# A transformer block on one core: gate and up of the last but one tile as whole matmuls, TensorE's instruction blocks in the planner's clock, and a rule row for each 64 banks

## The chip, the cores and the metric

The kernel runs on one core of a Trainium2 chip. The metric is the device time of one execution in microseconds, as the median of several runs. The profile is a recording of one execution; its lines name the engines PE (TensorE, with PEld for its weight loads), DVE (VectorE), ACT (ScalarE), POOL (GpSimd) and SP (SyncE, which issues the DMAs).

## The reference

One block of a transformer, with 2048 tokens of width 512, 32 heads of 16 columns and a feed-forward part of width 1792, all in bfloat16:

```python
mod = (silu(c) @ w_mod)                 # six rows of 512: sa, ca, ga, sb, cb, gb
h = layernorm(x) * (1 + ca) + sa
q, k, v = h @ wqkv                      # 32 heads, 16 columns each
p = softmax(q @ k.T / 4)                # 32 x 2048 x 2048 exponentials
x = x + ga * ((p @ v) @ wo)
h = layernorm(x) * (1 + cb) + sb
x = x + gb * ((gelu(h @ w_gate) * (h @ w_up)) @ w_down)
```

The 134 million exponentials are the bulk of what ScalarE does.

## The kernel before

**Tiling.** The queries are cut into seven sets (`SETS`): two of 512 tokens, three of 256 and two of 128. For every set the heads are taken in eight groups of four; for each group and each block of keys TensorE writes scores to a bank of PSUM, 128 keys by 512 columns (`qk`). A bank is the unit in which the kernel counts (`pos`). Six banks `ps_sc` hold scores, in two halves of three (`CH`). The bank `ps_pv` collects the product of the exponentials with the values (`pv_mms`), and `ps_mi` serves side work; late in the kernel the sixth score bank serves side work too (`bank`).

**Exponentials.** ScalarE turns two or three banks at a time into `E` (L369 in the profile). A part of the banks goes to VectorE: one `TENSOR_SCALAR` a bank writes the bits of an approximate power into `mreg` or `dreg`, and for four such banks three more operations on 2048 columns follow (`power_task`: mantissa, square, exponent); such a group is a "quad" in the code. Its product with the values takes two passes of 16 matmuls where a group of ScalarE's takes one.

**Side work.** Projections, the output projection with `wo`, the second normalisation and the feed-forward part of the sets that are done run on TensorE between the scores. With `split` set, `mm` writes a matmul of 128 weight columns as four of 32 columns, placed side by side on the array; with `whole` it stays one. Every matmul of the program is followed through two instructions, the weight load and the product. The last set but one (tile 14) is treated apart: `side_last` transposes its normalised rows (L354), then `side_raw` computes gate and up in eight chunks (`raw_chunk`), and VectorE copies each chunk from PSUM into `hreg`. GeLU, the product and the down projection of that tile follow behind the last exponential, in `tail`, beside the last tile's whole chain: sums, output projection, normalisation, gate, up, down. There gate and up of the last tile are whole matmuls already, since `tail` clears `split`.

**What sets the order.** No order is written out. The program is generated by a planner, `stream`, that keeps a clock of its own: `model` gives each operation a cost, and at every step the loop asks whether the next scores can start, whether a product with values is ready, whether side work is due and paid for (`credit`), or whether a filler matmul should run, one whose result isn't used. `plan` gives side work its windows, from `DUE` and the end of each set. Thresholds for all this stand in `RULES`, a row of nine numbers for a stretch of banks: readiness margin, the tolerated hole on VectorE, VectorE's allowed backlog, how far ScalarE may be ahead before scores go to VectorE alone, the columns that TensorE should have done in the last 3413 ns of the planner's clock (below that, fillers run), and so on. What the planner decides is then fixed in the program: each engine runs its own list in order and waits on semaphores for the others.

The model of a matmul, cut:

```python
cols, rows, tp = cost
mode = 0 if tp is None else (1 if rows == 32 else 2)
t = max(t, self.pe_issue)
if mode != self.pe_mode:
    t = max(t, self.pe_end + 105)
```

Of the kernel before, what the change touches and what calls it, by code (L numbers as in the profile page):

```python
# [21 lines left out]
NDC = D // P  # L22
NFC = F // P
NKT = S_TOK // P
# [8 lines left out]
QS = 2  # L33
PEN = {NSET - 2: (6, 7), NSET - 1: (5, 6, 7)}
NRAW = 8
CH = 3
SC = 2 * CH
NSL = 27
assert NSL % CH == 0
LEAD = 5  # L40
# [3 lines left out]
NEAR = 8  # L44
FIRST = 0
LAST = 3
FLOW = 4
DUE = (1054, 1420, 1597, 1802, -12, 0, -20)


def WIN(ends):
    due = DUE[:4] + (ends[5] + DUE[4], ends[5] - 16 + DUE[5], ends[6] + DUE[6])
    res = []
    for k in range(NSET - 2):
        s0 = max(ends[k] + 33, due[k - 1] if k else 0)
        res += [(s0, min(due[k], s0 + 15 * SETS[k][1] // P)), (s0, due[k])]
    return res + [(due[5], due[5]), (due[5], due[6])]
# [2 lines left out]
URGENT = 12  # L60
LATE = 2
RULES = (
# [16 lines left out]
)  # L79
END = (0, None)  # L80

# [13 lines left out]
_Rule = collections.namedtuple("_Rule", "ready hole back fill lag early alone ahead side2")  # L95


class _Op:
    __slots__ = ("eng", "stream", "seq", "fn", "inc", "waits", "clock", "tag", "t1")

    def __init__(self, eng, stream, seq, fn):
        self.eng = eng
        self.stream = stream
        self.seq = seq
        self.fn = fn
        self.inc = False
        self.waits = {}
        self.clock = None
        self.tag = None


class _Recorder:


    def __init__(self, nc):
        self.nc = nc
        self.ops = []
        self.count = {}
        self.bystream = {}
        self.clock = {e: {} for e in ALLENG}  # L120
        self.hist = {}
        self.pitch = {}
        self.kind = {}
        self.sem = {}
        self.dry = False
        self.split = False
        self.gelu = False
        self.probing = None
        self.free = {e: 700.0 for e in ALLENG}
        self.dma_free = self.pe_issue = self.pe_end = 0.0  # L130
        self.pe_mode = None
        self.tile_free = [0.0] * 16
        self.log = []

    def sb(self, name, shape, dt):
# [67 lines left out]
    def rec(self, eng, fn, reads=(), writes=(), dma=None, cost=0.0):  # L203

        if self.dry:
            return None
        stream = eng if dma is None else "d_" + dma
        seq = self.count.get(stream, 0) + 1
        needs = {}

# [70 lines left out]
    def model(self, op, t, cost):  # L281
        eng = op.eng
        if op.stream not in COMPUTE:
            size, run = cost
            self.free[eng] = t + 450
            self.dma_free = max(t + 900, self.dma_free) + size / (320 if run >= 1024 else 245 if run >= 512 else 200)
            op.t1 = self.dma_free + (1000 if run > 64 else 1500) + (1200 if self.split and size < 65536 else 0)
        elif eng == "pe":
            cols, rows, tp = cost
            mode = 0 if tp is None else (1 if rows == 32 else 2)  # L290
            t = max(t, self.pe_issue)
            if mode != self.pe_mode:
                t = max(t, self.pe_end + 105)
            q = range(16)
            if mode == 1:
                q = range(tp[0] // 8, tp[0] // 8 + 4)
            elif mode == 2:
                q = range(tp[1] // 32, 16, 4)
            t = max(t, max(self.tile_free[i] for i in q))
            end = t + max(cols, 64) / 2.4  # L300
            for i in q:
                self.tile_free[i] = end
            self.pe_mode, self.pe_issue, self.pe_end = mode, t + (4 if mode else 27), max(self.pe_end, end)
            self.free[eng] = t
            self.log.append((t, cols if mode == 0 else cols / 4))
            op.t1 = end + 158
        else:
            self.free[eng] = t + cost
            op.t1 = t + cost + (self.lag if eng == "act" else 92)
# [152 lines left out]
class _Kernel(_Recorder):  # L462
# [271 lines left out]
    def side_proj(self, col, g, fin):  # L734
# [5 lines left out]
        fin(mi)  # L740
        yield END

# [15 lines left out]
    def side_v(self, g, dc):  # L758
# [12 lines left out]
        self.done(("v", g, dc))  # L771
        yield END

    def side_t(self, src, n, h, out, mod):
# [9 lines left out]
        for i in range(2):  # L784
            dc = 2 * h + i
            self.modulate("dve", out(dc), pt[:, w * i:w * i + w], mod, dc)
        yield END

# [49 lines left out]
    def side_mod(self):  # L838
# [5 lines left out]
        for dst, k, s in ((self.ga, 2, 1.0), (self.gb, 5, 1.0)):  # L844
# [3 lines left out]
            self.ts("dve", dst[:, :], mi, s, None, ALU.mult)  # L848
            yield END
        for ci in range(0, 8, 2):  # L850
# [4 lines left out]
        if not self.dry:  # L855
            self.task([lambda qd=qd: self.tt("dve", self.wo[:, qd, :], self.wo[:, qd, :], self.ga[:, :], ALU.mult)
                       for qd in range(8)], "wo")
        yield END

# [5 lines left out]
    def side_wo_load(self):  # L865
# [7 lines left out]
        for j in range(4):  # L873
            for ee in range(2):
                src = self.A_wo.rearrange("(a j e r) n -> j e r a n", j=4, e=2, r=DH)[j, ee]
                self.dma("sp", self.wo[32 * j:32 * j + DH, ee:8:2, :], src, "wo%d" % (2 * j + ee))
        yield END

# [36 lines left out]
        self.tt("dve", self.xs[:, t, :], self.xs[:, t, :], self.xw, ALU.add)  # L915
        self.dma("sp", self.out[0, P * t:P * t + P, :], self.xs[:, t, :], "out%d" % (t % 4))

    def up_mm(self, bank, w, fc, c0, W, dci):
        self.mm(bank, self.up_w(w, fc, dci), self.t2T[:, dci, c0:c0 + W], start=(dci == 0), stop=(dci == NDC - 1))

    def near_end(self, k, qd, den):

# [35 lines left out]
    def side_ffn(self, gi, begin=False):  # L958
# [5 lines left out]
        prod = self.prodT if W == 512 else self.prodL  # L964
        flow = gi < FLOW
        kpb = 512 // W
# [89 lines left out]
    def raw_chunk(self, k, i, mi):  # L1056

        W, c0 = SETS[k][1], BCOL[k]
        x, f0 = i // 4, i % 4 * 4
        n = min(4, NFC - f0)  # L1060
        for s in range(n):
            for dci in range(NDC):
                yield W, lambda s=s, dci=dci: self.up_mm(
                    mi[:, W * s:W * s + W], (self.wg, self.wu)[x], f0 + s, c0, W, dci)
        dst = (self.gate5, self.up5)[x][:, f0:f0 + n, :]
        return lambda eng: self.copy(eng, dst, mi[:, 0:W * n].rearrange("p (k n) -> p k n", k=n))

    def side_raw(self, k):
        for i in range(NRAW):
            f = yield from self.raw_chunk(k, i, self.bank())  # L1070
            f("dve")
            self.done(("raw", k, i))
            yield END
# [134 lines left out]
    def stream(self):  # L1208
# [11 lines left out]
        rounds = []  # L1220
# [23 lines left out]
        pos = c = e = rp = loaded = 0  # L1244
# [8 lines left out]
        self.plain = dict(left)  # L1253
        quads = []
        wait = []
        cand = [k for k, (u, r, g0) in enumerate(rounds) if FIRST <= r < NKT * u[3] // 512 - LAST]
        self.begun = lambda u: group[u] <= cg
        quad = None

        def take(n):  # L1260
            r, i = [], pos
            while len(r) < n and i < nseq:
                if i not in vec:
                    r.append(i)
                i += 1
            return r, i

        def pick(q):
            used = [seq[m][2] for m in take(CH - 1)[0]]
            return next((q["rnd"][2] + j for j in q["j"] if j not in used), None)  # L1270

        def overdue():
            return {x[1][1] for x in self.tasks if x[1] is not None and x[1][0] == "shift" and self.plain[x[1][1]] <= LATE}
# [128 lines left out]

        early, late = self.weight_parts()
        while cg <= group[units[-1]]:
            self.rule = _Rule(*RULES[min(pos // 128, len(RULES) - 1)])
            parts = early or late
            if parts and pos >= loaded and (pos >= ends[FLOW - 1] + 8 if early else ("ffn", FLOW - 1) in self.have):
                parts.pop(0)()
# [3 lines left out]
            t = max(self.pe_now(), virt)  # L1412
# [4 lines left out]
            if c % 2:  # L1417
                self.two = self.fifth or (pos >= TWO_AT(ends) and self.credit > self.rule.side2)
            mem, after = take(CH - 1 if (left[units[1]] or self.two) and c % 2 else CH)
            s0 = CH * (c % 2)  # L1420
            if mem:
# [3 lines left out]
            if tq is not None and tq <= t + self.rule.ready:  # L1425
                slack = self.free["act"] - 600 - t
                w = self.next_side()
# [6 lines left out]
                if self.free["act"] > t + self.rule.alone and self.free["dve"] < t + 1500 and ("k", 3, 0) in self.have:  # L1434
                    alone = []
                    while len(alone) < CH:
                        if quad is None and not new_quad(overdue()):
# [43 lines left out]
                pos, e, c = after, e0 + n, c + 1  # L1481
# [4 lines left out]
            w = self.next_side()  # L1486
# [185 lines left out]
    def tail_rest(self, k, down):  # L1672
        q0, W = SETS[k]
        for i in range(NRAW, 8):
            gen = self.raw_chunk(k, i, self.scp[:, i % 3, :])
# [127 lines left out]
```

## Time and profile before

| what | value |
|---|---|
| median of three runs | 827.08 us (826.73 to 829.11) |
| the profiled execution | 827.44 us |
| its span, first to last instruction | 825.7 us |
| ScalarE busy | 795.3 us |
| VectorE busy | 754.5 us |
| TensorE busy | 753.6 us, 14256 matmuls |
| exponentials from scores on ScalarE | 451 of two banks, 246 of three |

The span is the time from the first instruction to the last; the execution's own time lies 1.74 us above it. A line of a group names the line of the program (often that of a helper), the engine, the operation, output and inputs by name, the shape and the number of instructions, then busy time in us and the mean of one in ns, and what ended the idle time before them. In a timeline a line gives the start in us, the length, and in brackets how long the engine had been idle and what it had waited for; "issue" means that it waited for nothing that the profile shows. Instructions of a group overlap, so that the mean of one may be longer than its share of the busy time.

### The profile page before, as it was taken

The page shows a single profiled execution, that of the slowest core. Times are in us where ns is not written, and L with a number is a line of the kernel's source. Part 1 is how long each engine was busy: PE and PEld are TensorE (multiplying, and loading weights), DVE is VectorE, ACT ScalarE, POOL GpSimd, SP SyncE. Part 2 cuts the span into 40 slices and gives each one's busy share as a digit, 9 for nine tenths or more (in the row PEclk, how much of TensorE's full clock was granted, in tenths as well). Part 3 has the DMA queues.
Part 4 walks back from the last instruction along what each step waited for, and adds up shares of the span by engine and source line. Part 5 has one row for each costly group of instructions (what it writes and reads, how often), then busy time and mean ns, then how long its engine had stood idle before and what let it go on. Part 6 is the DMA issues. An engine that isn't in the chain of part 4 may idle for free.

```text
span 825.7 us, 31347 instructions
## 1 busy us (share of the span) xinstructions
PE 753.6 (91%) x14256; PEld 303.8 (37%) x14256; DVE 754.5 (91%) x1359; ACT 795.3 (96%) x742; POOL 4.5 (1%) x13
## 2 busy tenths in 40 slices
PE   7999999989998998999898989998999999999977
PEld 3333333322222222222333333343543344465654
DVE  7866999999999999999998999999999999798755
ACT  6999999999999999999999999999999999999972
POOL 2000000000000000000000000000000000000000
PEclk9999999999999999999999999999999999999999
DMA  8101000000003211110003212111662433500000
GB/s 281 53 2 36 10 9 10 10 10 10 6 6 100 58 46 35 47 35 15 22 13 92 65 51 57 51 28 33 185 169 56 112 98 86 152 20 16 13 10 14
DMA packets 77215, 43.78 MB, mean 53 GB/s; under 512 B 21269, under 2 KB 75482, under 8 KB 77082
## 3 DMA queue, kind: packets, MB, share of 16 engines
q1 hardware_dynamic: 77080, 41.78, 18.4%
q8 instruction: 111, 1.82, 0.9%
q14 instruction: 22, 0.18, 0.1%
q10 hardware_dynamic: 2, 0.00, 0.0%
HBM read 39.15 MB, written 2.60 MB: 51 GB/s over the span
## 4 chain that ended last, share of the span: by engine, by line
ACT 83%; PE 11%; DVE 2%; DMA 1%; SPq 1%; issue 1%; DVEq 0%
ACT E L369 80%; PE ps_sc L350 6%; PE ps_mi L350 3%; ACT hreg L369 2%; PE ps_pv L350 1%; ACT L369 1%; SPq L419 1%; DMA xs<-in_A_x_dram 1%; DVE mreg L381 0%; DMA rb<-scr_rec 0%; DVE hreg L373 0%; DVE wreg L373 0%; DVE wreg L381 0%; DVE mreg L373 0%; DVE osb L390 0%
## 5 line engine op out<-in xcount | busy, mean ns | idle before, releaser
L369 ACT ACTIVATE E<-ps_sc 128x1024 bf16<-128x1024 f32 (+1 forms) x701 | 749.0, 1292 | 10.7 <-PE ps_sc L350 10.4
L350 PE MATMUL ps_sc<-qT,kmo 32*128 32x256 bf16 (+2 forms) x1728 | 199.2, 294 | 21.4 <-ACT E L369 17.8
L350 PE MATMUL ps_sc<-qT,kme 32*128 32x256 bf16 (+2 forms) x1728 | 195.5, 294 | 24.0 <-ACT E L369 18.6
L381 DVE TENSOR_SCALAR mreg<-ps_sc 128x512 uint16<-128x512 f32 x256 | 171.3, 686 | 11.9 <-PE ps_sc L350 9.9
L350 PE MATMUL ps_pv<-E,vaug 128*17 128x256 bf16 (+2 forms) x2720 | 148.5, 291 | 0.9 <-DVE osb L390 0.5
L350 PE MATMUL ps_mi<-wreg,mreg 128*32 128x256 bf16 (+2 forms) x1888 | 107.2, 325 | 4.9 <-DVE hreg L373 1.2
L350 PEld LDWEIGHTS ps_sc<-qT,kme 32*128 32x128 bf16 x1728 | 57.8, 92 | 142.4 <-ACT E L369 115.8
L350 PEld LDWEIGHTS ps_sc<-qT,kmo 32*128 32x128 bf16 x1728 | 58.6, 92 | 129.0 <-ACT E L369 106.8
L381 DVE TENSOR_SCALAR dreg<-ps_sc 128x512 uint16<-128x512 f32 x152 | 102.1, 686 | 3.1 <-PE ps_sc L350 1.7
L350 PEld LDWEIGHTS ps_pv<-E,vaug 128*17 128x17 bf16 x2720 | 53.8, 90 | 54.5 <-issue 38.0
L381 DVE TENSOR_SCALAR mreg<-mreg 128x2048 uint16<-128x2048 uint16 x96 | 65.0, 682 | 0.1
L350 PEld LDWEIGHTS ps_mi<-wreg,mreg 128*32 128x32 bf16 x1888 | 40.8, 95 | 46.5 <-issue 20.9
L350 PE MATMUL ps_pv<-mreg,vaug 128*17 128x256 bf16 (+2 forms) x816 | 48.0, 299 | 1.7 <-DVE mreg L373 1.0
L350 PE MATMUL ps_mi<-hreg,wreg 128*32 128x512 bf16 x480 | 38.5, 385 | 1.1 <-DVE vaug L390 0.9
L373 DVE TENSOR_TENSOR dreg<-mreg,dreg 128x2048 bf16<-128x2048 bf16 x32 | 38.9, 1216 | 0.1
L373 DVE TENSOR_TENSOR mreg<-dreg,mreg 128x2048 bf16<-128x2048 bf16 x32 | 38.7, 1211 | 0.1
L373 DVE TENSOR_TENSOR mreg<-mreg 128x2048 bf16<-128x2048 bf16 x32 | 38.8, 1212 | 0.0
L390 DVE CAST hreg<-ps_mi 128x512 bf16<-128x512 f32 (+1 forms) x50 | 33.8, 675 | 4.4 <-PE ps_mi L350 3.9
L350 PE MATMUL ps_mi<-xs,ident 128*32 128x512 bf16 (+2 forms) x424 | 33.1, 376 | 2.1 <-DMA xs<-in_A_x_dram 1.1
L350 PE MATMUL ps_mi<-wo,onorm 128*32 128x512 bf16 x448 | 33.6, 383 | 0.4 <-DVE onorm L373 0.2
L350 PE MATMUL ps_pv<-dreg,vaug 128*17 128x256 bf16 (+2 forms) x528 | 29.7, 290 | 3.0 <-DVE dreg L373 1.8
L373 DVE TENSOR_TENSOR hreg<-ps_mi,hreg 128x512 bf16<-128x512 f32 x44 | 30.2, 687 | 0.9 <-PE ps_mi L350 0.5
(170 smaller groups left out, 699.5 us busy)
## 6 DMA issues: line engine op xcount, KB each, us to landing
mreg<-in_B_w_up_dram SPq DMA_DIRECT2D x32, 256.0 KB, 3.0
mreg<-in_B_w_gate_dram SPq DMA_DIRECT2D x28, 256.0 KB, 3.4
mreg<-in_B_w_down_dram SPq DMA_DIRECT2D x16, 256.0 KB, 2.9
dreg<-in_B_w_down_dram SPq DMA_DIRECT2D x12, 256.0 KB, 3.3
mreg<-in_w_mod_dram SPq DMA_DIRECT2D x1, 2048.0 KB, 12.8
rb<-scr_rec SPq DMA_DIRECT2D x64, 32.0 KB, 1.9
out_dram<-xs SPq DMA_DIRECT2D x16, 128.0 KB, 1.7
rb<-scr_rec SPq DMA_DIRECT2D x104, 16.0 KB, 1.8
```

The lines of the kernel that those rows point to most:

```text
L350: return self.rec("pe", lambda e: e.matmul(out, lhsT, rhs, start=start, stop=stop, tile_position=tp), [lhsT, rhs, *after], [out], cost=(n, ...
L369: return self.rec("act", lambda e: e.activation(out, in_, func, scale=scale, **kw), rd, wr, cost=self.cost("act", out, [in_], "act") + load)
L373: return self.rec(eng, lambda e: e.tensor_tensor(out, a, b, op), [a, b], [out], cost=self.cost(eng, out, [a, b], "tt"))
L381: return self.rec(eng, lambda e: e.tensor_scalar(out, a, s1, s2, **kw), rd, [out], cost=self.cost(eng, out, [a], "ts") + (60 if len(rd) > ...
L390: return self.rec(eng, lambda e: e.tensor_copy(out, in_), [in_], [out], cost=self.cost(eng, out, [in_], "ts"))
L419: return e.dma_start(out, in_)
```

## The change

It has four parts.

1. `raw_chunk`, gate and up of tile 14 in the stream, asks for whole matmuls (`WHOLE`): one of 128 weight columns in place of four of 32.
2. The planner's clock counts TensorE's instructions, two for a matmul. At every 256 of them (`BLOCK`, the first after 63 have been counted ahead, `HEAD`) the next matmul may not start sooner than 3650 ns (`FETCH`) after the start of the block before.
3. `RULES` is read by `pos // 64` and not `pos // 128`, and its 16 rows become 31, most with new numbers.
4. The due time of tile 14's output projection is 34 banks earlier (`DUE`). `LASTW` is an empty table: the choice of groups for VectorE reads it, and falls back to `LAST` as before.

```diff
+WHOLE = True
+LASTW = {}
-DUE = (1054, 1420, 1597, 1802, -12, 0, -20)
+DUE = (1054, 1420, 1597, 1802, -12, -34, -20)
 RULES = (
-    (30, 450, 8, 4200, 1536, 400, 3200, 20, 1800),
+    (30, 50, 8, 2700, 1536, 400, 3200, 20, 1800),
+    (80, 100, 8, 4200, 1536, 400, 3200, 20, 2500),
...
+SEGB = 64
+HEAD, BLOCK, FETCH = 63, 256, 3650.0
...
+        self.pe_count, self.pe_block = HEAD, 0.0
...
             t = max(t, self.pe_issue)
+            self.pe_count += 2
+            if self.pe_count >= BLOCK:
+                self.pe_count -= BLOCK
+                t = self.pe_block = max(t, self.pe_block + FETCH)
             if mode != self.pe_mode:
...
-    def up_mm(self, bank, w, fc, c0, W, dci):
-        self.mm(bank, self.up_w(w, fc, dci), self.t2T[:, dci, c0:c0 + W], start=(dci == 0), stop=(dci == NDC - 1))
+    def up_mm(self, bank, w, fc, c0, W, dci, whole=False):
+        self.mm(bank, self.up_w(w, fc, dci), self.t2T[:, dci, c0:c0 + W], start=(dci == 0), stop=(dci == NDC - 1), whole=whole)
...
-                    mi[:, W * s:W * s + W], (self.wg, self.wu)[x], f0 + s, c0, W, dci)
+                    mi[:, W * s:W * s + W], (self.wg, self.wu)[x], f0 + s, c0, W, dci, WHOLE)
...
-        cand = [k for k, (u, r, g0) in enumerate(rounds) if FIRST <= r < NKT * u[3] // 512 - LAST]
+        cand = [k for k, (u, r, g0) in enumerate(rounds) if FIRST <= r < NKT * u[3] // 512 - LASTW.get(u[3], LAST)]
...
-            self.rule = _Rule(*RULES[min(pos // 128, len(RULES) - 1)])
+            self.rule = _Rule(*RULES[min(pos // SEGB, len(RULES) - 1)])
```

What the planner makes of it, first on TensorE, in the middle of tile 14's gate. `wreg` holds the transposed rows, `qT` and `hreg` by then hold weights of gate (the queries in that part of `qT` are used up), `ps_mi` and one bank of `ps_sc` collect the chunks, and rows with `kme` are scores. Before:

```order
L350 MATMUL ps_sc<-wreg,qT 32x128 x24
L350 MATMUL ps_mi<-wreg,qT 32x128 x8
L350 MATMUL ps_sc<-qT,kme 128x128 x12
L350 MATMUL ps_mi<-wreg,qT 32x128 x56
L350 MATMUL ps_sc<-wreg,qT 32x128 x8
L350 MATMUL ps_sc<-qT,kme 128x128 x8
L350 MATMUL ps_sc<-wreg,qT 32x128 x40
```

Now:

```order
L375 MATMUL ps_mi<-wreg,qT 128x128 x4
L375 MATMUL ps_sc<-wreg,qT 128x128 x5
L375 MATMUL ps_sc<-qT,kme 128x128 x8
L375 MATMUL ps_sc<-wreg,qT 128x128 x9
L375 MATMUL ps_sc<-qT,kme 128x128 x12
L375 MATMUL ps_sc<-wreg,qT 128x128 x2
L375 MATMUL ps_mi<-wreg,qT 128x128 x14
```

Between two groups of scores stand 9 to 16 whole matmuls where 40 to 64 narrow ones stood.

The second place is the end of the exponentials on ScalarE, up to the GeLU of tile 14 (`hreg<-hreg`). Before:

```order
L369 ACTIVATE E<-ps_sc 128x1024
L369 ACTIVATE E<-ps_sc 128x1536
L369 ACTIVATE E<-ps_sc 128x1024 x2
L369 ACT_TABLE_LOAD
L369 ACTIVATE hreg<-hreg 128x4x128 x3
```

Now:

```order
L394 ACTIVATE E<-ps_sc 128x1024
L394 ACTIVATE E<-ps_sc 128x1536
L394 ACTIVATE E<-ps_sc 128x512
L394 ACT_TABLE_LOAD
L394 ACTIVATE hreg<-hreg 128x4x128 x3
```

The exponentials end on a single bank where two of two banks stood. Over the whole program ScalarE has 1636 banks in place of 1640, 4 more go to VectorE, and TensorE has 468 matmuls fewer: 336 by the whole form and 136 fillers, with four more of the rest.

29 rows, old and new, of the table RULES are left out of this document.

## The prediction

> **What bounds the kernel now.** I read the page's busy times first, then busy time by stage, then who ScalarE waits for, then the instructions around those waits.
>
> ```profile
> span 825.7 us, 31347 instructions
> PE 753.6 (91%) x14256; PEld 303.8 (37%) x14256; DVE 754.5 (91%) x1359; ACT 795.3 (96%) x742; POOL 4.5 (1%) x13
> PEclk9999999999999999999999999999999999999999
> q8 instruction: 111, 1.82, 0.9%
> ACT 83%; PE 11%; DVE 2%; DMA 1%; SPq 1%; issue 1%; DVEq 0%
> ```
>
> ScalarE is busy for 96% and carries 83% of the chain that ended last. Three engines are above 90%, so the share alone doesn't say where time can be had. The stages do.
>
> ```profile
> 44.00:305.00 261.00, 239.70 (x3638) 76.37 (x3637) 242.78 (x400) 261.00 (x244) 0.31 (x1) 1.00 0.10 24
> 305.00:486.00 181.00, 164.37 (x2573) 53.55 (x2565) 175.99 (x292) 180.96 (x166) 0.00 (x0) 1.00 0.16 42
> 595.00:674.00 79.00, 73.89 (x1648) 33.88 (x1648) 76.72 (x141) 78.95 (x73) 0.00 (x0) 1.00 0.43 118
> ...
> 782.28:787.30 5.02, 3.92 (x175) 2.87 (x171) 4.30 (x9) 5.02 (x5) 0.00 (x0) 1.00 0.06 5
> 787.30:804.24 16.94, 12.97 (x585) 9.88 (x588) 7.53 (x16) 11.82 (x11) 0.00 (x0) 1.00 0.05 11
> 804.24:825.70 21.46, 16.19 (x191) 10.40 (x179) 11.69 (x29) 6.73 (x13) 0.00 (x0) 1.00 0.04 13
> ```
>
> The columns are stretch, length, then busy time of PE, weight loads, DVE, ACT and POOL. From 44 to 674 us ScalarE has no gap worth naming: only fewer or shorter exponentials could shorten it. From 787.30 to 804.24 it is busy 11.82 of 16.94 us, a gap of 5.1 us. After 804.24 the last tile's chain runs alone. The waits of ScalarE, first for 17 to 780 us, then for 786 to 804.3 us:
>
> ```profile
> ACT E L369 <- PE ps_sc L350: 2.3, 4, 0.8
> ```
>
> ```profile
> ACT E L369 <- PE ps_sc L350: 5.1, 6, 1.3
> ```
>
> So the place with something to win is the last 17 us of the exponentials, where ScalarE waits for scores. The timeline of ScalarE there, and TensorE's:
>
> ```profile
> 759.22 28.11 ACT L369 ACTIVATE E<-ps_sc 128x1024 bf16<-128x1024 f32 x28
> 788.24 2.46 ACT L369 ACTIVATE E<-ps_sc 128x1024 bf16<-128x1024 f32 x2 [0.91 <-PE ps_sc L350]
> ...
> 803.22 1.02 ACT L369 ACTIVATE E<-ps_sc 128x1024 bf16<-128x1024 f32 x1 [0.82 <-PE ps_sc L350]
> ```
>
> ```profile
> 783.76 0.69 PE L350 MATMUL ps_sc<-wreg,qT 128*32 128x128 bf16 x36
> ...
> 787.42 0.34 PE L350 MATMUL ps_mi<-wreg,qT 128*32 128x128 bf16 x9 [0.97 <-issue]
> 787.54 0.33 PE L350 MATMUL ps_sc<-wreg,qT 128*32 128x128 bf16 x8
> 787.80 0.40 PE L350 MATMUL ps_sc<-qT,kme 32*128 32x128 bf16 x8
> 788.13 0.74 PE L350 MATMUL ps_sc<-wreg,qT 128*32 128x128 bf16 x40
> 788.80 0.40 PE L350 MATMUL ps_sc<-qT,kme 32*128 32x128 bf16 x12
> 789.13 0.41 PE L350 MATMUL ps_sc<-wreg,qT 128*32 128x128 bf16 x16
> 789.37 0.62 PE L350 MATMUL ps_mi<-wreg,hreg 128*32 128x128 bf16 x32
> 789.92 0.28 PE L350 MATMUL ps_sc<-qT,kme 32*128 32x128 bf16 x3
> 791.17 0.34 PE L350 MATMUL ps_sc<-qT,kme 32*128 32x128 bf16 x5 [0.97 <-issue]
> ...
> 794.63 0.29 PE L350 MATMUL ps_mi<-wreg,mreg 128*32 128x128 bf16 x5 [1.02 <-issue]
> ...
> 798.66 0.34 PE L350 MATMUL ps_sc<-qT,kmo 32*128 32x128 bf16 x5 [1.24 <-issue]
> ...
> 802.40 0.23 PE L350 MATMUL ps_pv<-dreg,vaug 128*17 128x128 bf16 x3 [0.56 <-issue]
> ```
>
> TensorE stops five times for "issue", with no semaphore to wait for, even in the middle of a group of scores: 0.97 + 0.97 + 1.02 + 1.24 + 0.56 = 4.76 us. Between two stops 9+8+8+40+12+16+32+3 = 128 matmuls are issued, 256 instructions with their weight loads. The page counts 111 packets of instructions, 1.82 MB, so 16.4 kB each; the 14256 matmuls and as many loads make 28512/256 = 111 such blocks. TensorE starts again 3.75, 3.46, 4.03 and 3.74 us after the time before. A block of instructions therefore arrives every 3.75 us or so, and TensorE runs dry when it uses one up sooner: less the stops, it used these four up in 2.78, 2.44, 2.79 and 3.18 us, mean 2.80, or 21.9 ns a matmul with the changes between kinds.
>
> [...]
>
> **The change, part by part.**
>
> Gate and up of the last but one tile: 448 matmuls of 32 columns of weights become 112 whole ones. In the split form 36 take 0.69 us; with some 0.24 us for the first, that is 13 ns each, 52 ns for four. The whole form already stands in the last tile:
>
> ```profile
> 813.18 2.45 PE L350 MATMUL ps_sc<-wreg,qT 128*128 128x128 bf16 x41
> ```
>
> (2.45 − 0.22)/40 = 56 ns each. On the array the change costs 112 × 4 = 0.4 us; in instructions it takes away 336 matmuls and as many loads, 2.6 blocks.
>
> In the order shown with the change the scores stand between fewer, larger matmuls. From the transposes of the last but one tile (L354, at 782.28 us) to the last scores the order holds 705 matmuls before and 345 after, with 13 exponentials behind them in both.
>
> The worth of it, by the stretch from 782.28. Before: 705 × 21.9 ns = 15.4 us, plus 4.76 us of stops, is 20.2, and the last scores in fact started 20.5 us after the transposes:
>
> ```profile
> 802.78 0.40 PE L350 MATMUL ps_sc<-qT,kmo 32*128 32x128 bf16 x8
> ```
>
> After: 15.4 + 0.3 (what that sum missed) + 0.4 for whole matmuls, less 0.3 for 24 other matmuls fewer at 13 ns, is 15.8 us of array time. The blocks take 345/128 × 3.75 = 10.1 us beneath it, so no stop is left. To this come 0.4 us of scores and the last exponential, which has one bank now, 0.5 us: 16.7 us. ScalarE's own end would come sooner. Ten of the 13 exponentials fill the 11.8 us after 787.30; three stood before it, at 1.0 us each (28 in 28.11), so it began them at 784.3, 2.0 us after the transposes. Without gaps 13 take 13.1 us, and it would end 15.1 us after them. So what is late next is TensorE's array, and ScalarE still waits some 1.6 us. The later end, 16.7, against 804.24 − 782.28 = 22.0 gives −5.3 us. Ends: 0 if the stops don't come from the blocks, −6.9 if ScalarE alone sets the end. I take −5.3, since the stop repeats at exactly 128 matmuls.
>
> The rule table, one row for 64 banks of scores and not 128, the block model in the planner's clock, and the due time 34 banks earlier together only reorder work. What they change in ScalarE's work is counted in its order. The last exponential shrinks to one bank. Over the kernel there are 451 of two banks and 246 of three before (1640 banks), 456, 241 and one of one bank after (1636): one more round of four banks goes to VectorE.
>
> ```profile
> L369 ACT ACTIVATE E<-ps_sc 128x1024 bf16<-128x1024 f32 x451 | 444.3, 1144 | 7.0 <-PE ps_sc L350 6.8
> L369 ACT ACTIVATE E<-ps_sc 128x1536 bf16<-128x1536 f32 x246 | 358.5, 1574 | 1.2 <-PE ps_sc L350 1.2
> L381 DVE TENSOR_SCALAR mreg<-ps_sc 128x512 uint16<-128x512 f32 x256 | 171.3, 686 | 11.9 <-PE ps_sc L350 9.9
> L381 DVE TENSOR_SCALAR mreg<-mreg 128x2048 uint16<-128x2048 uint16 x96 | 65.0, 682 | 0.1
> L373 DVE TENSOR_TENSOR mreg<-mreg 128x2048 bf16<-128x2048 bf16 x32 | 38.8, 1212 | 0.0
> ```
>
> A bank is 1574 − 1144 = 430 ns of ScalarE; four are 1.7 us, of which 0.4 is in the 16.7 above already: −1.3 us elsewhere, with ScalarE full there. VectorE takes 4 × 0.686 + 2 × 0.682 + 1.212 = 5.3 us more. It hides in VectorE's gaps, 18.2 us in 44 to 305, 5.0 in 305 to 486, 2.3 in 595 to 674. Without that cover it would cost up to 5.3.
>
> The matmuls that only fill (xs with ident or nil) fall from 785 to 649. They are on no path while ScalarE is fed: worth 0, with the granted clock at 1.00 in every row above. Due time: 25 exponentials were left at the last but one tile's first output projection, 24 are in the new order, so the earlier window has moved nothing there: 0. DMAs are the same in number, 488 issues on SP in both orders. New gaps that the new table makes: the old one had 2.3 us from 17 to 780; I bound the change by −2.3 and +5, and take +1, since a new table has as many places to lose. The chain behind the last exponential has 235 matmuls, not 219: 16 × 13 ns = +0.2 us.
>
> Sum: −5.3 − 1.3 + 1.0 + 0.2 = −5.4. The profiled execution took 827.44 us, 1.74 outside its span, and the median of three runs is 827.08. From the median: 821.7.
>
> **The rivals.** The first is that the stops remain, as something other than blocks or because TensorE's array and its changes of kind set the pace: then only −1.3 + 1.2 remains, 827.0, no change. Against it speaks the count of exactly 128; for it, that the array's own time already ends later than ScalarE's, 16.7 against 15.1 us.
>
> The second ends slower: VectorE becomes the bound. It holds a score bank until it has read it, and the next scores wait for that bank.
>
> ```profile
> PEld ps_sc L350 <- DVE mreg L381: 4.9, 13, 0.7
> ```
>
> Such a wait was at most 0.7 us, 13 times, and hidden. From 595 to 674 VectorE has only 2.3 us free, and this stage gets 53 banks of 216 in place of 49 of 210, 2.6 more than its share, or 0.65 × 5.3 = 3.4 us. That is over by 1.1 us there. It decides when more than 5.4 + 2.5 = 7.9 us reach ScalarE, eleven or twelve waits of 0.7 more: about 830.5. The other stages have room, which speaks against it.
>
> The third is half a gain: blocks run short ahead of the transposes. The 742 matmuls there take 742/128 × 3.75 = 21.7 us of blocks and stand beside 23 exponentials, some 23 us at 1.0 each. If the stock is empty by then, two or three stops of 1 us stay: 824.3.
>
> **How the numbers follow.** Forecast 0.65, stops remain 0.13, VectorE 0.12, half gain 0.10. A measurement of this kernel can tell 0.3%, 2.5 us, from no change. The forecast and half gain are faster (under 824.6) but for a few hundredths: 0.74. The first rival is the same: 0.14. Slower: 0.12. The forecast's own range is 818 (ScalarE alone sets the end of the stretch, and half of the old gaps go too) to 824.5; to leave out no more than 2 in 10 the range must take in the first rival: 818 to 827.5.
>
> **What would show it.** Right: in the last 20 us of the exponentials ScalarE waits 2 us or less in sum, "issue" no longer stops TensorE between scores, and ScalarE's busy time falls by 1.7 us. Wrong: ScalarE's wait for scores from 17 to 780 us grows by more than 3 us, or stops at every 128 matmuls remain before the last scores, or a clock under 1.00.

## The result

The changed kernel takes 821.11 us (median of 11 runs, 819.32 to 825.31), the kernel before beside it 827.25 us (826.52 to 830.05): a ratio of 0.9928, with a 95% interval of 0.991 to 0.9947. The forecast was 821.7 us.

The page of the changed kernel:

```profile
span 823.0 us, 30418 instructions
PE 752.0 (91%) x13786; PEld 302.8 (37%) x13788; DVE 756.9 (92%) x1366; ACT 793.5 (96%) x743; POOL 4.6 (1%) x13
PEclk9979999999999999999999999999999999999999
q8 instruction: 108, 1.77, 0.9%
ACT 75%; PE 19%; DVE 5%; issue 0%; DMA 0%; DVEq 0%
```

ScalarE is 1.8 us less busy, VectorE 2.4 us more, three blocks of instructions are gone, and "issue" is down from 1% of the chain to 0%. One thing is new: the granted clock isn't full in the third slice. The profiled execution took 824.7 us, one of the slower ones; a second profile, from the run beside other kernels below, has a span of 819.0 us. The stretch from the transposes of tile 14 to the last exponential, and what follows it, by stage:

```profile
785.27:801.13 15.86, 15.75 (x386) 12.10 (x388) 11.64 (x26) 15.46 (x15) 0.00 (x0) 1.00 0.06 10
801.13:823.00 21.87, 16.36 (x217) 10.76 (x203) 11.62 (x28) 6.73 (x13) 0.00 (x0) 1.00 0.04 14
```

The stretch lasts 15.86 us in place of 21.96, and ScalarE waits in it only twice, for 0.18 and 0.22 us, as its timeline shows (the 0.18 of the first line lies ahead of the transposes):

```profile
783.46 4.20 ACT L394 ACTIVATE E<-ps_sc 128x1024 bf16<-128x1024 f32 x4 [0.18 <-PE ps_sc L375]
787.88 6.57 ACT L394 ACTIVATE E<-ps_sc 128x1024 bf16<-128x1024 f32 x6 [0.22 <-PE ps_sc L375]
794.63 6.50 ACT L394 ACTIVATE E<-ps_sc 128x1536 bf16<-128x1536 f32 x6 [0.18 <-PE ps_sc L375]
```

The three parts add up: the transposes begin 785.27 − 782.28 = 3.0 us later, the stretch is 6.1 us shorter, the rest 0.4 us longer, −2.7 in all, 825.7 to 823.0. In the second profile the transposes begin at 781.26, 1.0 us sooner than before, and the other two parts are the same: −6.7.

Why they began later in the first one stands in ScalarE's timeline near 45 us:

```profile
39.20 4.84 ACT L394 ACTIVATE E<-ps_sc 128x1024 bf16<-128x1024 f32 x4 [0.27 <-PE ps_sc L375]
45.60 1.02 ACT L394 ACTIVATE E<-ps_sc 128x1024 bf16<-128x1024 f32 x1 [1.55 <-PE ps_sc L375]
47.12 1.45 ACT L394 ACTIVATE E<-ps_sc 128x1536 bf16<-128x1536 f32 x1 [0.50 <-PE ps_sc L375]
49.49 1.02 ACT L394 ACTIVATE E<-ps_sc 128x1024 bf16<-128x1024 f32 x1 [0.92 <-PE ps_sc L375]
50.98 1.02 ACT L394 ACTIVATE E<-ps_sc 128x1024 bf16<-128x1024 f32 x1 [0.48 <-PE ps_sc L375]
52.50 2.86 ACT L394 ACTIVATE E<-ps_sc 128x1024 bf16<-128x1024 f32 x3 [0.49 <-PE ps_sc L375]
```

From 44 to 52.5 us ScalarE waits 3.9 us for scores. The stages there, with the granted clock as the third number from the end:

```profile
36.00:40.00 4.00, 3.37 (x32) 1.14 (x28) 3.48 (x17) 3.73 (x4) 0.00 (x0) 0.74 0.00 0
40.00:44.00 4.00, 4.00 (x33) 1.43 (x29) 2.33 (x6) 3.88 (x4) 0.00 (x0) 0.50 0.00 0
44.00:48.00 4.00, 3.67 (x57) 1.44 (x57) 1.41 (x2) 1.95 (x3) 0.00 (x0) 0.50 0.00 0
48.00:52.00 4.00, 4.00 (x61) 1.82 (x49) 1.53 (x3) 2.61 (x3) 0.00 (x0) 0.55 0.01 4
```

TensorE's clock was a half from 37.9 to 51.6 us, within the first and the last of these stages. It is full in the same stages of the second profile, which all read 1.00 (there it was a half from 19.1 to 22.5 us only):

```profile
36.00:40.00 4.00, 2.67 (x27) 0.95 (x27) 3.78 (x18) 4.00 (x5) 0.00 (x0) 1.00 0.00 0
40.00:44.00 4.00, 3.27 (x37) 1.26 (x37) 3.25 (x10) 4.00 (x4) 0.00 (x0) 1.00 0.00 0
44.00:48.00 4.00, 3.50 (x92) 1.64 (x93) 1.79 (x3) 3.55 (x4) 0.00 (x0) 1.00 0.02 4
48.00:52.00 4.00, 3.88 (x50) 1.75 (x52) 3.29 (x6) 3.94 (x6) 0.00 (x0) 1.00 0.01 2
```

### The profile page after: what moved, and what is told of

The parts are those of the page before. It is cut to its first block, busy times and chain, and to the rows that moved or that the text cites. A ratio compares the mean times of both kernels' runs of the same rounds, so it can differ in the third digit from the quotient of the medians.

```text
span 823.0 us, 30418 instructions
## 1 busy us (share of the span) xinstructions
PE 752.0 (91%) x13786; PEld 302.8 (37%) x13788; DVE 756.9 (92%) x1366; ACT 793.5 (96%) x743; POOL 4.6 (1%) x13
## 4 chain that ended last, share of the span: by engine, by line
ACT 75%; PE 19%; DVE 5%; issue 0%; DMA 0%; DVEq 0%
ACT E L394 73%; PE ps_sc L375 9%; PE ps_mi L375 7%; PE ps_pv L375 3%; ACT hreg L394 2%; DVE mreg L406 1%; ACT L394 1%; DVE dreg L406 1%; PE ps_mi L379 0%; DMA xs<-in_A_x_dram 0%; DVE st L434 0%; DVE hreg L415 0%; DVE mreg L398 0%; DVE wo L422 0%; DVE wreg L398 0%
## 5 line engine op out<-in xcount | busy, mean ns | idle before, releaser
L375 PE MATMUL ps_sc<-qT,kme 32*128 32x256 bf16 (+2 forms) x1728 | 193.1, 295 | 22.0 <-ACT E L394 18.6
L406 DVE TENSOR_SCALAR mreg<-mreg 128x2048 uint16<-128x2048 uint16 x100 | 67.8, 683 | 0.2
L375 PEld LDWEIGHTS ps_mi<-wreg,mreg 128*32 128x32 bf16 (+1 forms) x1872 | 41.9, 96 | 42.3 <-issue 18.8
L375 PE MATMUL ps_pv<-mreg,vaug 128*17 128x256 bf16 (+2 forms) x856 | 50.7, 298 | 2.4 <-DVE mreg L398 1.7
L398 DVE TENSOR_TENSOR mreg<-mreg 128x2048 bf16<-128x2048 bf16 x36 | 43.6, 1216 | 0.1
L415 DVE CAST hreg<-ps_mi 128x512 bf16<-128x512 f32 x49 | 33.6, 686 | 2.1 <-PE ps_mi L375 1.6
L398 DVE TENSOR_TENSOR dreg<-mreg,dreg 128x2048 bf16<-128x2048 bf16 x27 | 32.7, 1213 | 0.0
L375 PE MATMUL ps_mi<-wo,onorm 128*32 128x512 bf16 x416 | 31.0, 383 | 1.1 <-DVE wreg L398 0.5
L406 DVE TENSOR_SCALAR dreg<-dreg 128x2048 uint16<-128x2048 uint16 x44 | 29.9, 680 | 0.0
L375 PE MATMUL ps_mi<-mreg,hreg 128*32 128x512 bf16 x352 | 28.8, 384 | 0.0
```

The source lines that it names most:

```text
L375: return self.rec("pe", lambda e: e.matmul(out, lhsT, rhs, start=start, stop=stop, tile_position=tp), [lhsT, rhs, *after], [out], cost=(n, ...
L398: return self.rec(eng, lambda e: e.tensor_tensor(out, a, b, op), [a, b], [out], cost=self.cost(eng, out, [a, b], "tt"))
L406: return self.rec(eng, lambda e: e.tensor_scalar(out, a, s1, s2, **kw), rd, [out], cost=self.cost(eng, out, [a], "ts") + (60 if len(rd) > ...
L415: return self.rec(eng, lambda e: e.tensor_copy(out, in_), [in_], [out], cost=self.cost(eng, out, [in_], "ts"))
```

## The experiments

After the result there were two questions: which part of the change shortened the stretch, and what made the clock fall. Theory one: whole matmuls alone, because they need fewer blocks of instructions. Rivals: the rule table, the planner's knowledge of the blocks, or the form of the matmul. Theory two: the fillers that the new table lost held the clock. Rival: it fell for some other reason, and they are as idle as the prediction took them to be.

**Whole matmuls alone.** The kernel before, with one edit:

```diff
-    def up_mm(self, bank, w, fc, c0, W, dci):
+    def up_mm(self, bank, w, fc, c0, W, dci, whole=False):
...
-                    mi[:, W * s:W * s + W], (self.wg, self.wu)[x], f0 + s, c0, W, dci)
+                    mi[:, W * s:W * s + W], (self.wg, self.wu)[x], f0 + s, c0, W, dci, True)
```

> The kernel before with gate and up of the last but one tile as whole matmuls, and nothing else; its order differs from before in the last stretch alone. If the stops come from blocks of 128 matmuls, the stops between scores after 782 us go, and the time is 821.5 to 822.5 us, 5 us less than before. If the gain comes from the rules or the planner's clock, it stays above 826 us.

Measured: 821.98 us, ratio 0.9918 (0.9894 to 0.9942). Busy time from the transposes to the end of the exponentials, and ScalarE's timeline over it:

```profile
782.11:798.34 16.23, 15.58 (x380) 11.88 (x376) 11.23 (x24) 16.13 (x15) 0.00 (x0) 1.00 0.08 10
```

```profile
754.82 43.51 ACT L369 ACTIVATE E<-ps_sc 128x1024 bf16<-128x1024 f32 x42 [0.68 <-PE ps_sc L350]
798.35 1.28 ACT L369 ACT_TABLE_LOAD   x1
```

No gap is left from 754.82 to the end of the exponentials: 16.23 us in place of 21.96, and no "issue" stops TensorE there. This one edit gives what the whole change gives, as far as the intervals tell: a ratio of 0.9918 against 0.9928.

**Two halves.** The kernel before, with each of those matmuls as two of 64 columns of weights at places 0 and 64, 224 in all.

```diff
+        if whole == 2 and self.split:
+            for j in range(2):
+                self.mm(out[64 * j:64 * j + 64], lhsT[:, 64 * j:64 * j + 64], rhs, start, stop, (0, 64 * j), 3)
+            return
...
```

> The kernel before with gate and up of that tile as two matmuls of 64 columns of weights each: 224 instead of 448 or 112. By the blocks, 481 matmuls of the stretch take 14.1 us of blocks beneath some 15.7 us of array, so the stops go nearly as they do with whole ones: 822 to 823 us. If the form of the matmul sets the gain, half of it comes: 824 to 825 us.

Measured: 822.88 us, ratio 0.9928 (0.9901 to 0.9956). The stretch:

```profile
783.49:800.02 16.53, 16.21 (x536) 12.79 (x536) 11.69 (x25) 16.34 (x15) 0.00 (x0) 1.00 0.08 11
```

16.53 us, again with no wait of ScalarE. With half of the instructions of gate and up taken away nearly all of the gain has come. That fits a threshold in the count, and not a price by the form.

**The rule table alone, and the whole change with narrow matmuls.** The first is the changed kernel with narrow matmuls and without the block model, the second keeps the block model.

```diff
-WHOLE = True
+WHOLE = False
...
-            self.pe_count += 2
-            if self.pe_count >= BLOCK:
-                self.pe_count -= BLOCK
-                t = self.pe_block = max(t, self.pe_block + FETCH)
```

> The new rule table and due time alone: narrow matmuls, no block model. By the block theory the stops stay (about 5 us of waiting after 782 us); four banks fewer on ScalarE give 1.7 us, and the clock falls to a half near 40 us in some executions, since the fillers of the first 40 us are gone: 825 to 829 us. If the rule table carries the gain, 821 to 823 us.

```diff
-WHOLE = True
+WHOLE = False
```

> The changed kernel with narrow matmuls for gate and up of the last but one tile; rules, due time and block model as changed. By the block theory the stops return, since 336 matmuls more need 9.8 us more of blocks: 825 to 830 us. If the planner's knowledge of the blocks feeds ScalarE without whole matmuls, 822 to 824 us.

Measured: 830.08 us, ratio 1.0008 (0.9988 to 1.0027), and 829.78 us, ratio 1.0022 (1.0007 to 1.0036). The stops of TensorE are back, in the table's kernel:

```profile
791.79 0.57 PE L371 MATMUL ps_sc<-wreg,qT 128*32 128x128 bf16 x26 [1.36 <-issue]
795.81 0.55 PE L371 MATMUL ps_sc<-wreg,hreg 128*32 128x128 bf16 x14 [1.40 <-issue]
```

From the first to the second, by the lines of this timeline, stand 26 + 28 + 8 + 36 + 4 + 12 + 14 = 128 matmuls again. And the stops are back in the one whose planner knows the blocks (the two lines are 512 matmuls apart, four times 128):

```profile
789.76 0.38 PE L375 MATMUL ps_sc<-qT,kme 32*128 32x128 bf16 x10 [1.13 <-issue]
...
804.47 0.40 PE L375 MATMUL ps_pv<-E,vaug 128*17 128x128 bf16 x16 [1.12 <-issue]
```

In the latter ScalarE waits 2.7 us in the stretch, less than the 4.8 us of the table's kernel. But its stop at 804.47 now falls among the products with values that the last tile's chain needs, and this chain starts later, as ScalarE's wait for its statistics shows (1.22 us in the changed kernel):

```profile
810.64 0.60 ACT L394 ACTIVATE xs<-ps_sc 128x512 bf16<-128x512 f32 x1 [4.45 <-DVE st L434]
```

So the stretch and what follows it have to be taken together, in us of each profile:

| kernel | transposes to last exponential | behind it | sum |
|---|---|---|---|
| before | 21.96 | 21.46 | 43.42 |
| new table, narrow matmuls | 20.53 | 23.31 | 43.84 |
| new table and block model, narrow matmuls | 18.43 | 25.10 | 43.53 |
| before with two halves | 16.53 | 21.48 | 38.01 |
| before with whole matmuls | 16.23 | 22.16 | 38.39 |
| changed | 15.86 | 21.87 | 37.73 |

Neither the table nor knowledge of the blocks shortens the sum while 336 matmuls too many are in the stretch: what is won ahead of the last exponential is lost behind it. The due time was never changed apart from the table. Both narrow kernels also have the mean clock at 0.985 to 0.998, and their times follow it; in both profiles it was a half for 3.4 us of the stretch too, from 795.9 and from 792.0 us.

**The block model beside whole matmuls.** With the old table (the kernel before, whole matmuls and the model), and with the new one (the changed kernel without the model).

```diff
...
+            self.pe_count += 2
+            if self.pe_count >= BLOCK:
+                self.pe_count -= BLOCK
+                t = self.pe_block = max(t, self.pe_block + FETCH)
...
```

> The kernel before with whole matmuls and with the block model in the planner's clock, old rule table. If the block model only reorders a stretch that no longer runs dry, within 0.7 us of whole matmuls alone. If knowing the blocks is what lets the planner feed ScalarE, 1.5 us or more below it.

```diff
-            self.pe_count += 2
-            if self.pe_count >= BLOCK:
-                self.pe_count -= BLOCK
-                t = self.pe_block = max(t, self.pe_block + FETCH)
```

> The changed kernel without the block model in the planner's clock: the order differs in the last stretch alone. If the block model only reorders, within 0.7 us of the changed kernel; if knowing the blocks helps, 1.5 us or more slower; if it misleads the planner, as beside whole matmuls with the old table (823.4 against 822.0 us), 1.4 us faster.

Measured: 823.44 us with it (0.9933, 0.991 to 0.9957) against 821.98 without; 823.36 us without it (0.9935, 0.9913 to 0.9956) against 823.55 for the changed kernel beside it. It gains nothing in either pair; in the first it may cost 1.4 us, more than the 0.7 us allowed for mere reordering, but the intervals overlap and the second pair shows no difference. From the transposes to the end the two profiles of the first pair take the same 38.4 us, so what it may cost lies ahead of them.

**Fillers made thin.** The kernel before, its order untouched; the 108 fillers among the first 600 matmuls are 8 columns wide in place of 512, so they keep the place and lose the load.

```diff
...
+        o, r = (out[:, 0:8], rhs[:, 0:8]) if self.thin and self.count.get("pe", 0) < 600 else (out, rhs)
-        return self.rec("pe", lambda e: e.matmul(out, lhsT, rhs, start=start, stop=stop, tile_position=tp),
+        return self.rec("pe", lambda e: e.matmul(o, lhsT, r, start=start, stop=stop, tile_position=tp),
...
+                    self.thin = True
                     fill()
+                    self.thin = False
```

> The kernel before, in which the fillers among the first 600 matmuls (108) are 8 columns wide in place of 512; the planner doesn't know, and the order is the same. They compute nothing that is used. If these fillers hold the clock, it falls to a half for some 10 us near 40 us in most executions and the time rises by 3 to 5 us, to 830 to 833 us. If they hold nothing, 827 to 828.5 us as before.

Measured: 832.37 us, ratio 1.0061 (1.0048 to 1.0073), mean clock 0.981 to 0.988 in every execution, against 0.996 to 1.0 of the kernel before beside it. The stages by clock:

```profile
20.00:30.00 10.00, 10.00 (x98) 3.67 (x102) 4.71 (x11) 8.17 (x8) 0.00 (x0) 0.54 0.25 99
30.00:40.00 10.00, 7.98 (x151) 3.32 (x137) 9.32 (x35) 10.00 (x9) 0.00 (x0) 0.80 0.01 2
40.00:50.00 10.00, 9.36 (x143) 3.62 (x141) 5.70 (x13) 7.35 (x8) 0.00 (x0) 0.69 0.01 2
```

It falls twice, the first time earlier than expected, near 20 us. With nothing else changed the load of these fillers is worth 4.4 us. The changed kernel has 40 such fillers among its first 600 matmuls. And the kernel before isn't free of falls: of its 63 executions beside the runs of this section three have a mean clock of 0.994 or less, and they took 832.3 to 832.8 us.

**Load put back.** The changed kernel with hidden matmuls by zeros, 512 columns, added into the place of a product with values just ahead of it; the planner doesn't know of them. First 84, within the first 700 matmuls, then 32 (the 240th to the 420th), then 44 (up to the 420th).

```diff
...
+                if op is not None and not first and self.count["pe"] < PAD:
+                    self.pad(op, acc[32 * j:32 * j + VW, 0:W], j, src[j][:, W * kk:W * kk + W])
...
+    def pad(self, op, out, j, src):
+        f = op.fn
+        op.fn = lambda e: (e.matmul(out, self.nil[:, 0:VW], src, start=False, stop=False,
+                                    tile_position=(0, 32 * j)), f(e))[1]
```

> The changed kernel, in which 84 of the first products with values carry one more matmul each, by a matrix of zeros, 512 columns, added to the same place, unknown to the planner; all within the first 700 matmuls, where the new table has lost 72 fillers. If the lost fillers let the clock fall to a half near 40 us, the clock stays at 0.997 or above in nearly all executions, ScalarE's 3.7 us of waiting between 44 and 53 us goes, and the time is 819 to 820.5 us with a smaller spread. If the clock falls for another reason, the spread stays (819 to 825 us), and the added matmuls cost up to 1 us.

> The changed kernel with 32 hidden matmuls by zeros, only on products with values between the 240th and the 420th matmul, some 24 to 40 us, where TensorE was least busy before the clock fell. If the load just before the fall decides and 32 are enough, the clock stays at 0.996 or above and the time is 819 to 821 us, below the changed kernel. If the fall needs more load or an earlier one, the clock still falls in about half of the executions and the time is 820 to 826 us.

> The changed kernel with 44 hidden matmuls by zeros, on the products with values up to the 420th matmul: those of the run with 32, and the earlier ones. If the load up to the fall decides, the clock is at 0.996 or above in all executions and the time 820 to 821.5 us, steadier than the changed kernel. If 32 had already all that can be had, or the added matmuls delay the first scores, 821 to 824 us with the clock still between 0.99 and 1.

Measured: 823.0 us (0.9948, 0.9936 to 0.996) with 84, 821.48 (0.9919, 0.9891 to 0.9946) with 32, 821.64 (0.9931, 0.9909 to 0.9953) with 44. The mean clock was 0.996 to 1.0 with 84 and with 44, and 0.992 to 1.0 with 32, where it was a half from 17.7 to 31.3 us of the profiled execution. With 44 the stages are full again:

```profile
40.00:44.00 4.00, 3.35 (x43) 1.28 (x41) 3.39 (x11) 4.00 (x5) 0.00 (x0) 1.00 0.01 4
44.00:48.00 4.00, 3.46 (x90) 1.51 (x89) 2.04 (x3) 3.55 (x4) 0.00 (x0) 1.00 0.00 0
```

The load holds the clock, as theory two has it: 0.996 or above in all twelve executions with 84 and with 44, against nine of 19 of the changed kernel. But the time of 819 to 820.5 us didn't come. In the profile with 84 ScalarE waits 2.7 us for scores from 16 to 60 us, where the added matmuls run, against 1.9 us in the second profile of the changed kernel. It waits another 1.7 us from 700 to 781 us, behind stops of TensorE for "issue" of 0.32, 0.59 and 0.72 us, which the second profile doesn't have. They look like ends of blocks, which 84 matmuls more put in other places; that is argued, not tested. None of the three is clearly below the changed kernel.

**The changed kernel and whole matmuls alone, side by side.** Both again, unedited.

> The changed kernel again, beside the others: 819.5 to 825 us, in two groups by the granted clock (about 820.5 at 0.997 and above, about 824.5 at 0.99 and below).

> The kernel before with whole matmuls alone, again, beside the changed kernel: 821 to 823 us with the clock at 0.999 or above. If the new rule table were worth its 1.7 us of ScalarE's work, the changed kernel would lie below it; if the clock takes that back, they agree within 1.5 us.

Measured: 823.55 us (0.9937, 0.9912 to 0.9962) and 822.62 us (0.9925, 0.9899 to 0.9952), on the same chip. The 19 executions of the changed kernel, of both occasions, go by the mean clock: nine at 0.997 or above took 819.3 to 822.2 us, median 820.5; seven at 0.990 or below 824.1 to 826.1, median 825.3; three between them 822.4 to 823.0. Whole matmuls alone stay at 0.999 or above and within 821.1 to 823.4 us. So by the medians the new table saves some 1.5 to 2 us beyond whole matmuls with the clock up; in ten of the 19 executions the clock takes that back, in seven of them more than that.

## Why the prediction was right, and where it was not

The time, its sign and the place were right: 821.11 us against 821.7, and the gain lies in the stretch that was named. That the median came so close is in part luck: with the clock up the kernel takes 820.5 us, with a long fall 825.3, and the eight executions taken later have a median of 823.55. By its steps:

- **Blocks of 256 instructions stop TensorE.** Shown. Halves gain nearly as much as whole matmuls, narrow ones bring the stops back under the new table too, and the packets fell from 111 to 108, as 2 × 13788/256 = 107.7 says. The trace also has the instruction packets themselves, of 16384 bytes each: the five stops of the stretch in the kernel before end 1.33 to 1.43 us after one has landed, and those of the two narrow kernels 1.26 to 1.50 us after one. The next packet starts 1.1 to 1.6 us after TensorE goes on, and takes 0.9 to 1.5 us; these three make up the 3.5 to 4.0 us of a block.
- **The stretch, −5.3 us.** It was −6.1 (−5.7 for whole matmuls alone). The term that was mis-sized is the array's time, worked out as 15.8 us to the last scores. In the changed kernel these start at 799.80, 14.5 us after the transposes, in the kernel with whole matmuls alone 14.8 us after them. The 21.9 ns a matmul came from blocks in which other short waits may have lain; no run takes that apart. So ScalarE, not the array, sets the end of the stretch now: the 1.6 us of waiting that was to remain was 0.4 us.
- **Four banks fewer, −1.3 us outside the stretch, and +1.0 us for new gaps.** Together −0.3. With the clock up the transposes came 1.0 us sooner, with the clock down 3.0 us later. The reason for the allowance, that a new table has as many places to lose, was no mechanism: the first profile lost its time with the clock.
- **Fillers, 0 us.** This step failed. They were called worth nothing while ScalarE is fed, "with the granted clock at 1.00 in every row above". But a clock of 1.00 in the old rows is what those fillers had bought: with all 108 of the first 600 matmuls made thin the kernel before takes 4.4 us more. The two errors, 0.8 us too little in the stretch and some 4 us unseen in a part of the executions, partly cancel in the median.
- **The chain behind, +0.2 us.** It was +0.4: the last products with values end 0.85 us after the last exponential in place of 0.50, and ScalarE's wait for the last tile's statistics is 1.22 us in place of 0.86.
- **The rivals.** The stops did not remain, and ahead of the transposes the profile after has one of 0.22 us, at 782.59. VectorE took its added work without a wait that mattered: 77.95 of 79 us from 595 to 674 in the profile after, and one wait of ScalarE of 0.5 us there. As a sign of error the forecast had named ScalarE's waits from 17 to 780 us growing by more than 3 us; they grew by 2.4 us, to 4.7, but the clock under 1.00, its other sign, did come.

## What to carry to other kernels

Look for "issue" gaps that recur at a fixed number of instructions, here at every 128 matmuls with their weight loads. TensorE used a block up in 2.44 to 3.18 us and started again 3.46 to 4.03 us after the time before, so what counted in this stretch was instructions, and the whole form, 56 ns for four narrow ones of 13 ns, made it 5.7 us shorter (21.96 to 16.23 us). Before work that is not used by anything is priced at nothing, ask which state it keeps: a resource that shows no trouble in the old profile may do so because of it, as the clock did here (0.996 to 1.0 with these fillers, 0.981 to 0.988 and 4.4 us more with thin ones). And when a change has several parts, run the parts alone: here one of the four did all that the intervals can tell.

## What the runs showed of the hardware that was not expected

The clock fell to a half although TensorE had not been idle for long. Busy time from 24 to 36 us, ahead of the fall, in the kernel before:

```profile
24.00:36.00 12.00, 11.13 (x185) 3.85 (x182) 9.89 (x29) 12.00 (x11) 0.00 (x0) 1.00 0.02 6
```

in the changed kernel, and its longest wait of TensorE's matmuls there:

```profile
24.00:36.00 12.00, 9.63 (x155) 3.24 (x152) 9.82 (x28) 12.00 (x12) 0.00 (x0) 1.00 0.02 5
```

```profile
PE ps_sc L375 <- ACT E L394: 2.2, 6, 0.6
```

Thirty matmuls fewer of 185, and no wait over 0.6 us, went ahead of a half clock of 13.7 us; the longest wait in the kernel before was 0.2 us there. Between the two kernels the load differs, 11.13 against 9.63 us busy of 12, and the waits with it; which of the two decides is not shown apart.

That the same program falls at one place in one execution and not in the next shows in its two profiles. The same stretches, in the first profile and then in the second:

```profile
15.68:19.10 3.42, 1.65 (x36) 0.55 (x24) 3.28 (x10) 3.42 (x4) 0.00 (x0) 1.00 1.09 371
19.10:22.51 3.41, 3.20 (x39) 1.21 (x39) 2.60 (x13) 3.41 (x4) 0.00 (x0) 1.00 1.01 405
34.52:37.93 3.41, 2.26 (x24) 0.64 (x25) 3.30 (x17) 3.41 (x4) 0.00 (x0) 1.00 0.00 0
37.93:51.58 13.65, 13.32 (x141) 5.27 (x141) 6.58 (x16) 9.82 (x9) 0.00 (x0) 0.50 0.00 1
```

```profile
15.68:19.10 3.42, 1.61 (x32) 0.55 (x24) 3.28 (x10) 3.42 (x4) 0.00 (x0) 1.00 1.10 355
19.10:22.51 3.41, 3.39 (x25) 0.61 (x25) 2.57 (x12) 2.74 (x3) 0.00 (x0) 0.50 1.02 404
34.52:37.93 3.41, 2.17 (x26) 0.55 (x22) 3.24 (x18) 3.41 (x4) 0.00 (x0) 1.00 0.00 0
37.93:51.58 13.65, 12.01 (x189) 5.09 (x190) 10.25 (x25) 13.14 (x13) 0.00 (x0) 1.00 0.01 2
```

After nearly equal work the clock fell at 37.93 in the first and not in the second, and at 19.10 in the second and not in the first. In the fourteen traces of this case the falls inside a program last 3.41, 10.24, 13.65 or 17.07 us, and where there are several they begin whole multiples of 3.41 us apart (17.07 us with thin fillers; 450.56 us in the first profile, where a second one begins at 488.49). So in these traces the lengths of the falls and the distances between them are whole multiples of 3.41 us, and the same program fell first at 37.93 us in one execution and at 19.10 us in the other. Laid out from the falls in steps of 3.41 us, the thin place near 36 us fills one step in the first profile, and a fall followed; in the second it is divided between two steps, and none followed.

How thin is an estimate made after the fact from the traces of the kernel before and of the changed kernel: each matmul that starts in a step is counted by its columns times the part of the array that its rows and columns take, the 17 columns of a product with values as the 32 of their place. So counted, the steps ahead of the two falls of the first profile held the work of 21 and 22 whole matmuls of 128 columns (from 34.52 to 37.93 us, and from 485.08 us). In the second the steps around the first of these places held 24 and 27. Of the other steps at a full clock, those that held 24 or fewer are one in the first profile, with 22, and two in the kernel before, with 22 and 24; the steps there are laid out from the fall behind its last instruction, at 827.27 us. So the count nearly parts them, and not fully. Time busy alone parts them less: 2.47 of 3.42 us came before a fall in the changed kernel without the block model, and 2.08 did not in the kernel before, from 14.90 us. No run set a load to test this count.
